# The second forward factor of a global filter network: cosine and sine products in sixteen 32x32 tiles, two steps a run

## The chip, the cores and the metric

One core of a Trainium2 chip runs the whole program. The metric is the device time of one execution in microseconds (us). Three runs of the kernel before gave 2619.46, 2620.3 and 2620.4 us; the median is 2620.3 us.

## What is computed

The reference, cut to what matters, for 8 batches of 3008 tokens with 256 channels:

```python
X = np.fft.rfft(x, axis=1)                 # x: (8, 3008, 256)
Y = X * (filt_r + 1j * filt_i)[None]       # 1505 frequencies x 256 channels
y = np.fft.irfft(Y, n=3008, axis=1)
h = y.reshape(24064, 256) @ w_in           # 256 -> 2048
g = np.where(h > 0, h, np.exp(np.minimum(h, 0)) - 1)
out = g @ w_out                            # 2048 -> 256
```

So every batch passes through a frequency filter (forward transform, product with a complex filter, inverse transform) and then through two dense layers with an ELU between them. All of it is in 32-bit floats.

## The kernel before

**The transform.** 3008 is 47 times 64. The forward transform has a first factor over 64 points (`a_unit`) and a second over 47 points (`b_unit`); the inverse has the second factor back (`bi_unit`) and the first back (`n_unit`). Between the factors the data goes through DRAM to be laid out anew: `z_write` and `z_read` before `b_unit`, `y_write` and `y_read` after `bi_unit`. The second factor works on 32 columns of the first, four at a time, so there are 8 steps g of a batch (`NG` = 8). The cosine and sine parts are folded: 24 rows of sums and 24 rows of differences for each of two parts.

**A `b_unit` of before.** One step g. Sixteen matmuls with weights of 48 rows x 32 columns (`fb`) write the real part into the PSUM bank `psr` and the imaginary one into `psi`. The 48 rows hold a cosine and a sine product that the matmul itself adds. VectorE then multiplies with the filter straight out of PSUM (`products`, L328 to L331, four instructions of 128x512), and GpSimd adds and subtracts the results (L385 to L390). After every second step comes a `bi_unit` over both: 16 matmuls of 24 rows x 32 columns with 512 moving columns, one for each 32x32 tile of the array (`tile_position`), into all four banks (`pv`), which ScalarE copies out (L412).

**The dense layers.** They run by Strassen's scheme, with 7 instead of 8 products. An item is a quarter of the hidden width for one group of tokens; there are 8 x 6 x 4 = 192. Its seven up-steps (`s1`, `s2`, `s6`, `s5`, `s7`, `s3`, `s4`, line L494) multiply with `w_in`, its seven down-steps (L576) with `w_out`. Each step is two fp32 matmuls of 256 columns, which the trace shows as four records.

**The order of the work is written by hand.** The loop runs over quads i. Quad i holds the up-steps of item i and the down-steps of item i-1, interleaved by a string of U and D:

```python
for k in "UUDUDDU":                       # "DUUDUDDU" if i in opens
    ...
for fn, a in plan.get((i, 0), ()):        # place 0: the middle of the quad
    fn(*a)
for k in "DUUDUDD":                       # "DUUDUD" if i in opens
    ...
for fn, a in plan.get((i, 1), ()):        # place 1: its end
    fn(*a)
```

The transform of the next batch is put into this stream by `at(quad, place, fn, ...)`. Below, "quad n" is a quad's place within a batch's 24 (`PER`), that is `t + n` in the code. Every engine takes its instructions in this order.

Before, the eight `b_unit`s stand at the ends of quads 9, 10, 12, 13, 15, 16, 18 and 19, the `bi_unit`s at the ends of 11, 14, 17 and 20. A quad in `opens` begins with a down-step; these were quads 3, 5, 8, 12, 15, 18 and 21. Other work in place 0 or 1 that matters here: `c_unit` (four more VectorE sums of a finished group, L592) in place 0 of quads 5, 9, 13, 17 and 21; `o_unit` (two VectorE transposes, L614) in place 0 of quads 6, 10, 14, 18 and 22; `n_unit` in place 0 of quads 8, 12 and 16. At the end of quads 12, 16 and 20 a finished group adds three VectorE sums (L592).

**PSUM.** Four banks (`po`) hold the down-steps' sums. The other four go round in a list, `banks`:

```python
banks = [0, 1, 2, 3]

def bank(name, shape=(P, 2, D)):
    i = banks.pop(0)
    return i, psM.tile(list(shape), FP32, tag="m%d" % i, name=name)
```

Whoever takes a bank waits until all reads of its last content are done. An item takes its first bank in `s1` (key "s"), a second in `s2` (key "a"), a third in `s7` (key "d"). `s7`'s result is read by VectorE (`add("b22", ...)`, L502 with `phd`), and `s4` then accumulates onto the same bank, so it waits for that read.

Of the kernel before, what the change touches and what calls it, by code (L numbers as in the profile page):

```python
# [11 lines left out]
FP32 = mybir.dt.float32  # L12
U32 = mybir.dt.uint32
AXT = mybir.ActivationFunctionType
# [12 lines left out]
P = 128  # L27
# [14 lines left out]
def _make_tables():  # L42
# [53 lines left out]

    fb, bb = np.zeros((P, 2, 2, 32)), np.zeros((P, 2, 4, 32))
    for r in (LO, HI):  # L100
        fb[r, :, 0, :24] = gb[r, :, 0:24]
        fb[r, 0, 1, 1:24] = gb[r, 0, 24:47]
        fb[r, 1, 1, :24] = gb[r, 1, 24:48]
    for o in range(0, P, 32):
        for p, (t, c) in enumerate(((gr, 0), (gr, 24), (gi, 0), (gi, 24))):
            bb[o:o + 24, 0, p, :24] = t[0:24, 0, c:c + 24]

    bb[0:24, 1, 0, :24], bb[0:24, 1, 1, :24] = gr[0:24, 1, 0:24], gr[24:48, 1, 24:48]
    bb[0:24, 1, 2, :24], bb[0:24, 1, 3, :24] = gi[24:48, 1, 0:24], gi[0:24, 1, 24:48]
    pairs = np.concatenate([fb.reshape(P, P), bb.reshape(P, 2 * P)], 1)  # L110
    lie = np.concatenate([2 * np.arange(24), 2 * np.arange(24) + 1])
    gb[:, :, lie] = gb[:, :, :48].copy()
    for t in (gr, gi):
# [15 lines left out]
def kernel(  # L129
# [16 lines left out]
    def pool(name, bufs, **kw):  # L146
        return ctx.enter_context(tc.tile_pool(name=name, bufs=bufs, **kw))
# [4 lines left out]
    sdp = pool("sdp", 2)  # L152
    tnp = pool("tnp", 2)
    t1p = pool("t1p", 3)
    t2p = pool("t2p", 2)
    sp = pool("sp", 1)
    qp = pool("qp", 1)
    t3p = pool("t3p", 1)
# [5 lines left out]
    psO = pool("psO", 1, space=PSUM)  # L164
    psM = pool("psM", 1, space=PSUM)

    pairs = glob.tile([P, 3 * P], FP32, name="pairs")
    fb = pairs[:, 0:P].rearrange("p (v c k) -> p v c k", v=2, c=2)
    bb = pairs[:, P:3 * P].rearrange("p (v a i) -> p v a i", v=2, a=4)

    w_in, w_out = ([glob.tile([P, 7, 2, P], FP32, name="%s%d" % (n, i)) for i in range(4)] for n in ("wi", "wo"))

    fbufs = [glob.tile([P, 2, 2, D], FP32, name="f%d" % i) for i in range(FBUFS)]
    edges = glob.tile([P, 2], FP32, name="edges")
    fd = fdp.tile([NG, 2, 48, 2, 2, D], FP32, name="fd")
    fp = fdp.tile([NG, 4, 24, 2, 2, D], FP32, name="fp")

    xs, tas, tns, t1s, t2s, ss, t3s, t4s, zs, yds, ys, g_of, po_of, cs_, sds = ({} for _ in range(15))

    def raw(src, row, ap, col=0):  # L180
        return bass.AP(tensor=src.tensor, offset=src.offset + row * D + col, ap=ap)
# [98 lines left out]

    def t_first(g):

        pool, tag = (t4p, "t4") if g % 4 > 1 else (t2p, "t2")
        t = t2s[0, g] = pool.tile([P, 4, D], FP32, tag=tag, name="t2")
        for j in range(2):
            i = j + 2 * (g % 2 if g < 4 else 0)
            ps = psO.tile([P, 2, 256], FP32, tag="po%d" % i, name="po%d" % i)
            for u in range(2):
                k = 4 * g + 2 * j + u
                for dh in range(2):  # L290
                    nc.tensor.transpose(ps[0:ROWS, u, ts(dh, P)], zt[k // 16][dh][:, ts(k % 16, ROWS)], eye)
            nc.scalar.activation(out=t[0:ROWS, 2 * j:2 * j + 2, :], in_=ps[0:ROWS], func=AXT.Copy)
# [10 lines left out]
            nc.sync.dma_start(z[r], t[HALVES[r]])  # L303

    def z_read(b, g):
        t = t2s[b, g] = t2p.tile([P, 4, D], FP32, tag="t2", name="t2")
        for p, r in enumerate((0, 24, 64, 88)):
            k = p * K2 + 4 * g
            nc.sync.dma_start(t[r:r + 24].rearrange("i u d -> i (u d)"), zs[b][:, k:k + 4, :].rearrange("i u d -> i (u d)"))

    def f_read_first(g, t):
        for a, r in enumerate((LO, HI)):
            nc.gpsimd.dma_start(t[r].rearrange("p c u d -> p (c u d)"), fd[g, a].rearrange("q c u d -> q (c u d)"))

    def f_read(b, g):
        t = fbufs[(b * NG + g) % FBUFS]
        for a in range(4):
            nc.gpsimd.dma_start(t[32 * a:32 * a + 24].rearrange("p c u d -> p (c u d)"),
                                fp[g, a].rearrange("q c u d -> q (c u d)"))
# [47 lines left out]


    def b_unit(b, g):
        t = t2s.pop((b, g))  # L370
        f = fbufs[(b * NG + g) % FBUFS]
        (i0, re), (i1, im) = (bank(n) for n in ("psr", "psi"))
        for c in range(2):
            for a in range(4):
                for ps, k in ((re, LO), (im, HI)):
                    nc.tensor.matmul(ps[32 * a:32 * a + 32, c, :], fb[k, 1 if g == a == 0 else 0, c, :], t[k, a, :],  # L376
                                     start=True, stop=True)
        sr, si = (sp.tile([P, 2, D], FP32, tag=n, name=n) for n in ("sr", "si"))
        if g % 2 == 0:
            ss[b, g] = qp.tile([P, 4, 2, D], FP32, tag="z", name="zs")  # L380
        z = ss[b, g - g % 2][:, :, g % 2]
        p, q = z[:, 0:2], z[:, 2:4]
        products(re, im, f, sr, si, p, q)
        banks.extend((i0, i1))
        nc.gpsimd.tensor_tensor(out=sr, in0=sr, in1=p, op=ALU.add)  # L385
        nc.gpsimd.tensor_tensor(out=p[:, 0], in0=sr[:, 0], in1=sr[:, 1], op=ALU.add)
        nc.gpsimd.tensor_tensor(out=p[:, 1], in0=sr[:, 0], in1=sr[:, 1], op=ALU.subtract)
        nc.gpsimd.tensor_tensor(out=si, in0=si, in1=q, op=ALU.add)
        nc.gpsimd.tensor_tensor(out=q[:, 0], in0=si[:, 0], in1=si[:, 1], op=ALU.subtract)
        nc.gpsimd.tensor_tensor(out=q[:, 1], in0=si[:, 0], in1=si[:, 1], op=ALU.add)  # L390
        if g == 0:

            nc.gpsimd.tensor_copy(out=p[0:32], in_=sr[0:32])
            for i in range(2):
                nc.gpsimd.tensor_copy(out=q[0:32, i], in_=si[0:32, 1 - i])

# [233 lines left out]
    def w_fetch(k, queue=nc.gpsimd):  # L632
        q, j = divmod(k, 4)

        if k in (3, 4):
            wd = t2p.tile([P, 4, D], FP32, tag="t2", name="wd").rearrange("p u d -> p (u d)")
        elif k in (10, 11):
            wd = t1p.tile([P, XC, D], FP32, tag="t1", name="wd").rearrange("p u d -> p (u d)")
        elif k in (6, 7, 8, 9):
            wd = xp.tile([P, 2, 2, D], FP32, tag="xc", name="wd").rearrange("p k u d -> p (k u d)")  # L640
        else:
            wd = fbufs[{5: 0, 12: 1, 13: 2, 14: 0, 15: 1}.get(k, k)].rearrange("p c u d -> p (c u d)")
        wd = wds[k] = wd.bitcast(U32).rearrange("p (a w) -> p a w", w=2)
        if j < 2:
            srcs = [moe_w_in.bitcast(U32)[ts(j, P), ts(q, 1024)]]
        else:
            srcs = [moe_w_out.bitcast(U32)[ts(4 * q + 2 * (j - 2) + i, P), :] for i in range(2)]
        for i, s in enumerate(srcs):
            n = 512 // len(srcs)
            queue.dma_start(wd[:, ts(i, n), :].rearrange("p a w -> p (a w)"), s)  # L650
# [79 lines left out]
    def f_pairs(c, u):  # L730

        src = fd.rearrange("g a q c u d -> (g a) q c u d")[:, :, c, u, :]
        dst = fp.rearrange("g (a u) k c h d -> (g a) u k c h d", u=2)[:, u, :, c, :, :]
        nc.gpsimd.dma_start(dst[:, :, 0, :], src[:, 0:48:2, :])
        nc.gpsimd.dma_start(dst[:, 1:24, 1, :], src[:, 1:46:2, :])
        nc.gpsimd.dma_start(dst[:, 0, 1, :], src[:, 47, :])
        if u == 0:
            nc.gpsimd.dma_start(dst[0, :, 1, :], src[0, 1:48:2, :])

    with tc.manual_schedule():  # L740


        with tc.tile_pool(name="boot", bufs=1) as bp:
# [3 lines left out]
            gs = bp.tile([P, 3, 2, 64], FP32, name="gs")  # L747
            gr, gi = gs[:, 1], gs[:, 2]
            zq = qp.tile([P, 4, 2, D], FP32, tag="z", name="zq")
            pqs = [[(sp if i == 0 else bp).tile([P, 2, D], FP32, name="s%s" % n, **({"tag": "s" + n} if i == 0 else {}))  # L750
                    for n in "ri"] +
                   [zq[:, 0:2, i], zq[:, 2:4, i]] for i in range(2)]
            t3f = t3p.tile([P, 2, 4, D], FP32, tag="t3", name="t3")
            zt[0] += [bp.tile([P, 16 * ROWS], FP32, name="zt%d" % i) for i in range(2)]

# [114 lines left out]
        for c in range(2):  # L870
            for u in range(2):
                at(1 + 2 * c + u, 0, f_pairs, c, u)
        for i, f in enumerate(fbufs):
            at(3 + i, 1, nc.vector.memset, f, 0.0)
        for b in range(B):
            t = (b - 1) * PER
            if b > 0:
                for c, s in enumerate((2, 2, 4, 4, 7, 7)):
                    at(t + s, 0, x_unit, b, c)
                    if c % 2 == 0:  # L880
                        opens.add(t + s + 1)
                        at(t + s, 1, a_unit, b, c)
                    nb, nxt = (b, c + XBUFS) if c + XBUFS < NXC else (b + 1, c + XBUFS - NXC)
                    if nb < B:
                        at(t + s, 1, x_load, nb, nxt)
                    at(t + s, 1, z_write, b, c)
                for g in range(NG):
                    s = t + 9 + g + g // 2
                    at(s, 1, b_unit, b, g)
                    at(s - 2, 1, f_read, b, g)  # L890
                    at(s - 2, 1, z_read, b, g)
                    if g % 2:

                        opens.add(s + 2)
                        at(s + 1, 1, bi_unit, b, g - 1)
                        at(s + 1, 1, y_write, b, g - 1)
            for m, (s, place) in enumerate(((23, 0), (25, 1), (29, 1), (32, 0), (36, 0), (40, 0))):
                if b > 0 or m > 0:
                    at(t + s - 2, 0, tn_read, b, m)
# [8 lines left out]
        for i in range(-PER, len(items) + 3):  # L908
            ups, up_tail = up_steps(*items[i]) if 0 <= i < len(items) else ((), None)
            downs, down_tail = down_steps(*items[i - 1]) if 1 <= i <= len(items) else ((), None)  # L910
            ups, downs = list(ups), list(downs)
            for k in "DUUDUDDU" if i in opens else "UUDUDDU":
                s = ups if k == "U" else downs
                if s:
                    s.pop(0)()
            for fn, a in plan.get((i, 0), ()):
                fn(*a)
            for k in "DUUDUD" if i in opens else "DUUDUDD":
# [41 lines left out]
```

## Time and profile before

| | |
|---|---|
| profiled execution: span, its only time on the page | 2618.7 us |
| runs (three), median | 2620.3 us |
| TensorE matmul busy | 2569.9 us, 98% |
| VectorE busy | 1852.8 us, 71% |
| ScalarE busy | 1504.0 us, 57% |
| GpSimd busy | 486.9 us, 19% |
| TensorE clock granted | 0.994 of full on average |

PE is TensorE's matmul, PEld its weight load, DVE is VectorE, ACT ScalarE, POOL GpSimd, SP SyncE, which only issues DMAs. "L328" is line 328 of the kernel. Of the profiled execution the page gives the span and no other time; the runs' median lies 1.6 us above that span. The chain that ended last is the path of waits and work that set the end. Busy shares are means over the whole program: within a quad an engine can be much fuller.

### The profile page before, as it was taken

The page shows a single profiled execution, that of the slowest core. Times are in us where ns is not written, and L with a number is a line of the kernel's source. Part 1 is how long each engine was busy: PE and PEld are TensorE (multiplying, and loading weights), DVE is VectorE, ACT ScalarE, POOL GpSimd, SP SyncE. Part 2 cuts the span into 40 slices and gives each one's busy share as a digit, 9 for nine tenths or more (in the row PEclk, how much of TensorE's full clock was granted, in tenths as well). Part 3 has the DMA queues.
Part 4 walks back from the last instruction along what each step waited for, and adds up shares of the span by engine and source line. Part 5 has one row for each costly group of instructions (what it writes and reads, how often), then busy time and mean ns, then how long its engine had stood idle before and what let it go on. Part 6 is the DMA issues. An engine that isn't in the chain of part 4 may idle for free.

```text
span 2618.7 us, 41226 instructions
## 1 busy us (share of the span) xinstructions
PE 2569.9 (98%) x15300; PEld 2220.2 (85%) x15300; DVE 1852.8 (71%) x3203; ACT 1504.0 (57%) x2622; POOL 486.9 (19%) x669
## 2 busy tenths in 40 slices
PE   6799999999999999999999999999999999999998
PEld 4688889888898888988889888998889888898887
DVE  6876776677666776777667767677677667766666
ACT  7665555655555555555555555555555555555554
POOL 5102330024100331004300134002330023300000
PEclk9899999999999999999999999999999999999999
DMA  9544222432224232333314331143321332210010
GB/s 296 169 115 105 63 63 55 117 83 70 66 62 115 63 92 48 82 90 80 79 45 104 83 98 45 45 111 96 86 61 40 87 85 63 63 41 20 22 28 17
DMA packets 228840, 206.51 MB, mean 79 GB/s; under 512 B 130962, under 2 KB 194674, under 8 KB 228640
## 3 DMA queue, kind: packets, MB, share of 16 engines
q1 hardware_dynamic: 211328, 166.90, 25.4%
q0 software_dynamic: 15856, 36.25, 4.9%
q8 instruction: 121, 1.98, 0.3%
q10 hardware_dynamic: 1456, 0.72, 0.1%
q14 instruction: 79, 0.65, 0.1%
HBM read 131.91 MB, written 78.17 MB: 80 GB/s over the span
## 4 chain that ended last, share of the span: by engine, by line
PE 96%; DMA 0%; DVE 0%; ACT 0%; issue 0%; DVEq 0%; SPq 0%; ACTq 0%
PE po L576 44%; PE phs L494 25%; PE phd L494 12%; PE pha L494 6%; PE psn L443 3%; PE psr L376 2%; PE psa L228 2%; PE pv L409 1%; PE po L324 0%; DMA yd<-t 0%; PE psi L376 0%; DMA t<-yd 0%; PE psr L324 0%; DVE c L592 0%; PE psi L324 0%
## 5 line engine op out<-in xcount | busy, mean ns | idle before, releaser
L576 PE MATMUL po<-g,wo 128*128 128x256 f32 (+1 forms) x5376 | 1306.1, 376 | 0.0
L576 PEld LDWEIGHTS po<-g,wo 128*128 128x128 f32 x5376 | 1016.2, 190 | 139.1 <-issue 20.0
L505 ACT ACTIVATE g<-phs 128x512 f32<-128x512 f32 (+1 forms) x576 | 339.3, 589 | 819.2 <-PE phs L494 819.1
L502 DVE TENSOR_TENSOR g<-phd,g 128x512 f32<-128x512 f32 (+1 forms) x384 | 259.4, 675 | 413.3 <-ACT e L512 322.2
L512 ACT ACTIVATE e<-e 128x512 f32<-128x512 f32 (+1 forms) x768 | 477.2, 621 | 24.3
L516 DVE SCALAR_TENSOR_TENSOR g<-e,g 128x512 f32<-128x512 f32 (+1 forms) x576 | 400.5, 695 | 1.3 <-ACT e L512 1.3
L494 PE MATMUL phs<-y,wi 128*128 128x256 f32 (+1 forms) x1536 | 394.5, 380 | 0.0
L494 PE MATMUL phs<-ys,wi 128*128 128x256 f32 (+1 forms) x1536 | 387.9, 375 | 1.5 <-ACT g L505 1.5
L511 ACT ACTIVATE e<-g 128x512 f32<-128x512 f32 (+1 forms) x576 | 353.2, 613 | 35.7 <-DVE g L502 26.6
L494 PEld LDWEIGHTS phs<-y,wi 128*128 128x128 f32 x1536 | 284.9, 191 | 55.1 <-issue 11.5
L494 PEld LDWEIGHTS phs<-ys,wi 128*128 128x128 f32 x1536 | 291.9, 190 | 34.9 <-ACT g L505 2.5
L385 POOL TENSOR_TENSOR sr<-sr,zs 128x512 f32<-128x512 f32 x56 | 71.3, 1273 | 1131.7 <-DVE zs L330 1131.7
L516 DVE SCALAR_TENSOR_TENSOR g<-e,phs 128x512 f32<-128x512 f32 (+1 forms) x192 | 129.9, 677 | 128.5 <-ACT e L512 128.5
L511 ACT ACTIVATE e<-phs 128x512 f32<-128x512 f32 (+1 forms) x192 | 112.9, 588 | 147.7 <-PE phs L494 147.7
L494 PE MATMUL phd<-ys,wi 128*128 128x256 f32 (+1 forms) x768 | 194.6, 376 | 0.0
L494 PE MATMUL phd<-y,wi 128*128 128x256 f32 (+1 forms) x768 | 193.8, 375 | 0.0
L494 PE MATMUL pha<-y,wi 128*128 128x256 f32 (+1 forms) x768 | 193.8, 375 | 0.0
L494 PEld LDWEIGHTS phd<-ys,wi 128*128 128x128 f32 x768 | 145.4, 190 | 19.0 <-DVE g L502 3.0
L494 PEld LDWEIGHTS pha<-y,wi 128*128 128x128 f32 x768 | 146.1, 190 | 16.3
L494 PEld LDWEIGHTS phd<-y,wi 128*128 128x128 f32 x768 | 146.1, 190 | 16.2
L502 DVE TENSOR_TENSOR g<-pha,g 128x512 f32<-128x512 f32 (+1 forms) x192 | 129.2, 673 | 40.5 <-PE pha L494 40.2
L553 DVE TENSOR_TENSOR g<-g,g 128x512 f32<-128x512 f32 (+1 forms) x192 | 130.7, 681 | 6.7
(129 smaller groups left out, 2356.5 us busy)
## 6 DMA issues: line engine op xcount, KB each, us to landing
yd<-t SPq DMA_DIRECT2D x127, 192.0 KB
t<-yd SPq DMA_DIRECT2D x190, 128.0 KB
z<-t SPq DMA_DIRECT2D x84, 256.0 KB
f<-fp POOLq DMA_DIRECT2D x224, 96.0 KB, 3.1
t<-z SPq DMA_DIRECT2D x224, 96.0 KB
out_dram<-o SPq DMA_DIRECT2D x632, 32.0 KB
tn<-tn_t SPq DMA_DIRECT2D x48, 256.0 KB
xc<-in_x_dram SPq DMA_DIRECT2D x84, 128.0 KB
```

What stands on the lines that cost most here:

```text
L228: nc.tensor.matmul(p[o:o + 64, u, :], w[r, u, o:o + 64], src[r, u, :], start=True, stop=True)
L376: nc.tensor.matmul(ps[32 * a:32 * a + 32, c, :], fb[k, 1 if g == a == 0 else 0, c, :], t[k, a, :], start=True, stop=True)
L385: nc.gpsimd.tensor_tensor(out=sr, in0=sr, in1=p, op=ALU.add)
L443: nc.tensor.matmul(ps[:, ts(q, P)], t[:, i - 4 * m, ds(dh * P, P)], w[:, i - 4 * m, :], start=True, stop=True)
L494: nc.tensor.matmul(ps[:, a, 0:h], w_in[q][:, COMBO[n], a, :], y[n], start=start and a == 0, stop=True, skip_group_check=True)
L502: nc.vector.tensor_tensor(out=g[o], in0=i0, in1=i1, op=ALU.add)
L505: nc.scalar.activation(out=g[o], in_=i0, func=AXT.Copy)
L511: nc.scalar.activation(out=e, in_=src, func=AXT.Relu, scale=-1.0)
L512: nc.scalar.activation(out=e, in_=e, func=AXT.Exp, scale=-1.0)
L516: nc.vector.scalar_tensor_tensor(out=g[n], in0=es[n], scalar=1.0, in1=src, op0=ALU.subtract, op1=ALU.max)
L553: nc.vector.tensor_tensor(out=b12, in0=b22, in1=b12, op=ALU.subtract)
L576: nc.tensor.matmul(po[i][:, u, 0:h], w_out[q][:, COMBO[n], a, :], g[n][:, a, :], start=q == 0 and a == 0 and n in (1, 3, 6, 4), stop=True, ...
```

## The change

- `b_unit` now takes two steps g and g+1 in one run: 16 matmuls, each 24 rows x 32 columns on a tile of its own, with 512 moving columns (20 matmuls for the first pair, whose lone column has other weights). Cosine and sine products come out apart in four PSUM banks: c, s, ci, si. The pairs' units stand at the ends of quads 9, 12, 15 and 18.
- ScalarE copies c and si out; four VectorE instructions form c+s, c-s, si+ci and si-ci. For the first pair (g = 0) VectorE also copies one column out of each of the four banks. The banks go back into the list in the order c, si, s, ci.
- The products with the filter, now from SBUF, are eight VectorE instructions a pair instead of eight out of PSUM. `re_unit` does four of them and four GpSimd instructions in the quad after (10, 13, 16, 19), `im_unit` the other four and four in the quad after that (11, 14, 17, 20). Both stand in a new place 2, behind the third step of a quad.
- The quads after a `b_unit` and after a `bi_unit` are opened by a down-step: quads 10, 13, 16 and 19 join 12, 15, 18 and 21.
- The filter is read in pairs in place 0 of the quad before the unit, and `z_read` in pairs two quads before. `t2`, the filter buffers and `rs` become tiles of fixed place; 2 of the 3 filter buffers are used.

The core of the diff:

```diff
     def b_unit(b, g):
-        (i0, re), (i1, im) = (bank(n) for n in ("psr", "psi"))
-        for c in range(2):
-            for a in range(4):
-                for ps, k in ((re, LO), (im, HI)):
-                    nc.tensor.matmul(ps[32 * a:32 * a + 32, c, :], fb[k, 1 if g == a == 0 else 0, c, :], t[k, a, :],
-                                     start=True, stop=True)
...
-        products(re, im, f, sr, si, p, q)
-        banks.extend((i0, i1))
-        nc.gpsimd.tensor_tensor(out=sr, in0=sr, in1=p, op=ALU.add)
...
+        pf = [bank("pf") for _ in range(4)]
+        both = [(a, p, slice(1 if g == a == 0 else 0, 2), 0) for a in range(4) for p in range(4)]
+        if g == 0:
+            both = [(0, p, slice(0, 1), 1) for p in range(4)] + both
+        for a, p, js, v in both:
+            r = slice(32 * p, 32 * p + 24)
+            nc.tensor.matmul(pf[p][1][32 * a:32 * a + 32, js, :], fb[r, v, :], t2[r, js, a, :],
+                             start=True, stop=True, tile_position=(32 * p, 32 * a))
+        t = rs[b, g] = sp.tile([P, 4, 2, D], FP32, tag="r", name="r")
+        c, s, ci, si = (ps for _, ps in pf)
+        for k, ps in ((1, c), (3, si)):
+            nc.scalar.activation(out=t[:, k], in_=ps, func=AXT.Copy)
+        for k, ps in ((0, s), (2, ci)):
+            nc.vector.tensor_tensor(out=t[:, k], in0=t[:, k + 1], in1=ps, op=ALU.add)
+            nc.vector.tensor_tensor(out=t[:, k + 1], in0=t[:, k + 1], in1=ps, op=ALU.subtract)
+        if g == 0:
+            for k, ps in ((0, c), (1, s), (3, ci), (2, si)):
+                nc.vector.tensor_copy(out=t[0:32, k, 0, :], in_=ps[0:32, 0, :])
+        banks.extend(pf[p][0] for p in (0, 3, 1, 2))
+
+    def re_unit(b, g):
+        t, f = rs[b, g], fall[:, 0:2]
+        z = ss[b, g] = qp.tile([P, 4, 2, D], FP32, tag="z", name="zs")
         for c in range(2):
...
+            nc.vector.tensor_tensor(out=z[:, 2 + c], in0=t[:, c], in1=f[:, :, 0, c, :], op=ALU.mult)
+            nc.vector.scalar_tensor_tensor(out=z[:, c], in0=t[:, 2 + c], scalar=-1.0, in1=f[:, :, 1, c, :],
+                                           op0=ALU.mult, op1=ALU.mult)
+        for c in range(2):
+            nc.gpsimd.tensor_tensor(out=z[:, 2 + c], in0=z[:, 2 + c], in1=z[:, c], op=ALU.add)
+        for c, op in ((0, ALU.add), (1, ALU.subtract)):
+            nc.gpsimd.tensor_tensor(out=z[:, c], in0=z[:, 2], in1=z[:, 3], op=op)
...
+    def im_unit(b, g):
+        t, f, z = rs.pop((b, g)), fall[:, 0:2], ss[b, g]
+        for c in range(2):
+            nc.vector.tensor_tensor(out=t[:, c], in0=t[:, c], in1=f[:, :, 1, c, :], op=ALU.mult)
+            nc.vector.tensor_tensor(out=t[:, 2 + c], in0=t[:, 2 + c], in1=f[:, :, 0, c, :], op=ALU.mult)
+        for c in range(2):
+            nc.gpsimd.tensor_tensor(out=t[:, c], in0=t[:, c], in1=t[:, 2 + c], op=ALU.add)
+        for c, op in ((0, ALU.subtract), (1, ALU.add)):
+            nc.gpsimd.tensor_tensor(out=z[:, 2 + c], in0=t[:, 0], in1=t[:, 1], op=op)
...
-                for g in range(NG):
-                    s = t + 9 + g + g // 2
+                for g in range(0, NG, 2):
+                    s = t + 9 + 3 * g // 2
+                    opens.update((s + 1, s + 3))
+                    for k in (g, g + 1):
+                        at(s - 1, 0, f_read, b, k)
+                        at(s - 2, 1, z_read, b, k)
                     at(s, 1, b_unit, b, g)
...
+                    at(s + 1, 2, re_unit, b, g)
+                    at(s + 2, 2, im_unit, b, g)
+                    at(s + 2, 1, bi_unit, b, g)
+                    at(s + 2, 1, y_write, b, g)
...
-            for k in "DUUDUDDU" if i in opens else "UUDUDDU":
+            for n, k in enumerate("DUUDUDDU" if i in opens else "UUDUDDU"):
...
+                if n == 2:
+                    for fn, a in plan.get((i, 2), ()):
+                        fn(*a)
```

## The prediction

> **What bounds the kernel now.** I read the page's busy line and chain first, then the matmul timeline around a `b_unit` and a `bi_unit`, then VectorE's timeline in the quads that the change touches, the busy times quad by quad, and the waits.
>
> ```profile
> PE 2569.9 (98%) x15300; PEld 2220.2 (85%) x15300; DVE 1852.8 (71%) x3203; ACT 1504.0 (57%) x2622; POOL 486.9 (19%) x669
> ...
> PE 96%; DMA 0%; DVE 0%; ACT 0%; issue 0%; DVEq 0%; SPq 0%; ACTq 0%
> ```
>
> TensorE is the bound. So an edit is worth what it takes out of TensorE's stream, less every new wait in it, because TensorE's steps run in order. The units in that stream, batch 2 (g = 3, then the `bi_unit` after it):
>
> ```profile
> 593.11 1.89 PE L576 MATMUL po<-g,wo 128*128 128x256 f32 x8
> 594.92 0.40 PE L376 MATMUL psr<-t,pairs 48*32 48x256 f32 x1
> ...
> 595.95 1.13 PE L494 MATMUL phs<-y,wi 128*128 128x256 f32 x4
> 596.92 1.03 PE L494 MATMUL pha<-y,wi 128*128 128x256 f32 x4
> ...
> 606.41 1.89 PE L576 MATMUL po<-g,wo 128*128 128x256 f32 x8
> 608.23 1.14 PE L409 MATMUL pv<-zs,pairs 24*32 24x512 f32 x32
> 609.30 1.13 PE L576 MATMUL po<-g,wo 128*128 128x256 f32 x4
> 610.27 1.05 PE L494 MATMUL phs<-y,wi 128*128 128x256 f32 x4
> ```
>
> A step (x4) takes 0.863 us start to start, a quad of 14 steps 12.09. The two down-steps from 593.11 would end at 594.84; the next ordinary step starts at 595.95 and is 0.97 long instead of 0.863. One `b_unit` thus costs 1.11 + 0.11 = 1.22 us. By the same count the `bi_unit` costs 608.14 to 609.30 plus 0.11 = 1.27 us; that of a first pair, with 40 records, 1.42.
>
> VectorE runs behind TensorE. A `b_unit` of quad 9 (g = 0) and what VectorE does of it:
>
> ```profile
> 539.44 0.40 PE L376 MATMUL psr<-t,pairs 48*32 48x256 f32 x1
> ...
> 542.47 0.69 DVE L328 TENSOR_TENSOR sr<-psr,f 128x512 f32<-128x512 f32 x1
> ...
> 544.87 0.68 DVE L502 TENSOR_TENSOR g<-pha,g 128x512 f32<-128x512 f32 x1
> ```
>
> It comes to the unit only 3.03 us after the unit began, since the tail of the item before is queued ahead; four 128x512 instructions then take 2.40, 0.60 each. In the other quads the delay is longer. Busy times of quads 13, 16 and 17:
>
> ```profile
> 582.38:594.92 12.54, 12.54 (x64) 10.48 (x56) 12.28 (x22) 6.37 (x11) 6.11 (x6) 1.00 0.11 33
> ...
> 622.63:636.70 14.07, 14.07 (x80) 12.37 (x73) 9.20 (x16) 8.36 (x16) 5.33 (x6) 1.00 0.10 29
> 637.73:650.01 12.28, 12.28 (x65) 10.57 (x57) 11.90 (x22) 6.02 (x11) 7.19 (x9) 1.00 0.00 0
> ```
>
> The columns are length, then PE, PEld, DVE, ACT, POOL. VectorE's 71% hides two quads with `c_unit` that are already full: 12.28 of 12.54 and 11.90 of 12.28. In quad 13 TensorE already waits for it:
>
> ```profile
> 591.41 0.68 DVE L502 TENSOR_TENSOR g<-phd,g 128x512 f32<-128x512 f32 x1
> 592.14 1.13 PE L494 MATMUL phd<-ys,wi 128*128 128x256 f32 x4
> ...
> PEld phd L494 <- DVE g L502: 3.0, 8, 0.4
> ```
>
> `s4` was due at 591.97 and starts at 592.14, after the read of `s7`'s bank ends at 592.09.
>
> **The change, part by part**, for one batch, times 7 (batch 0 is filtered by other functions).
>
> *Tiling.* The new unit has the form of the `bi_unit` (16 tiles, 24x32, 512 columns), so I price it 1.27; its moving rows are two runs of 256 columns instead of one, and no row shows that to cost. The first pair has 20 matmuls, two of them on the same tile in four cases, as its `bi_unit` has: 1.42, up to 1.7 as they stand first. Before 8 x 1.22 = 9.76, after 3 x 1.27 + 1.42 = 5.23: a gain of 4.53, **-31.7 us** (-26 to -33).
>
> *Banks, first pair (quad 10).* The unit holds all four banks. `s1` of quad 10, behind one down-step, takes c's bank, and for g = 0 that bank has a last reader on VectorE: the one-column copy, queued behind the tail and the four sums. The copy starts 3.03 + 2.40 = 5.43 us after the unit's start and takes about 0.35 (estimate: 256-column sums take 0.42, start to start 0.34). `s1` can start at 5.8; without the wait it would at 1.23 (matmuls of a 40-record `bi_unit`) + 0.97 = 2.2. Everything behind `s1` stands for 3.6 us; the last copy (si, for `s2`'s bank) ends at 6.8, when `s1` is done. **+25.2 us** (23 to 27).
>
> *Banks, other pairs.* c and si have only ScalarE as a reader. It copies at 0.60 each and is free then: `bi_unit`'s copies wait 0.79 for the matmuls. `s1` comes one down-step later, as behind the `bi_unit`, where it starts on time (610.27). Cost 0; were that copy late, 0.6 for 21 units is 12.6. But a unit at the end of quads 12, 15 and 18, which end with only one down-step behind `s4`, now needs `s4`'s bank, whose reader ends at 581.45 for a unit due at 581.35: 0.15 x 3, **+3 us** (0 to 5).
>
> *VectorE.* A pair has 12 instead of 8 instructions of 128x512, 4 x 0.60 x 28 = 67 us in all. Where it is idle they are free: quad 16 has a hole of 4.01 us before `s7`'s sum, quads 10 and 19 enough. Quad 13: `add("b11")`, queued behind the four sums, ends 7.87 after the unit's start (589.22), `re_unit` adds 4 x 0.60 to 0.70 = 2.5, the `c_unit` takes 2.19 as now, the sum of `s7` 0.65: 13.2. `s4` is due at 1.07 + 0.11 + 12 x 0.863 = 11.53. The wait is 1.67 instead of 0.17, **+10.5 us** (5 to 14). Quad 17 loses the unit in front of it and gets `im_unit` for `products`, while quad 16 now opens with a down-step, so that its tail ends one step nearer to the boundary or past it. VectorE comes to `products` 4.1 us behind the stream now (L328 at 640.71, the steps end at 636.61), 0.86 later then (quad 12, opened so and with the same three sums, shows 586.23 against 581.26, 4.97): 4.96 + 0.6 + 2.45 + 2.2 + 0.65 = 10.86, against `s4` due at 11 x 0.863 = 9.5: 1.36, **+9.5 us** (3 to 14). Quads 11, 14 and 20 come out at 7.9 to 9.5: no wait.
>
> *GpSimd and `bi_unit`.* `im_unit`'s GpSimd work must end before the quad does, 12.18 us after its start. It begins when VectorE has two products, 5.9 (quads 11, 20), 6.1 (14), 6.8 (17), and takes 4 x 1.27 to 1.45, in a first pair 2 x 0.39 more: it ends between 11.0 and 12.4, and in quad 17 TensorE is late anyway. 0 (0 to 8). `re_unit`'s part has a quad of cover.
>
> *Moves at no cost.* Two more ScalarE copies a pair lie in holes (819 us before L505). The filter reads (8 issues of 0.50 on POOL's queue, landing in 3.1) now follow `im_unit` and have over 10 us. `z_read` goes ahead of a `y_write` on SP's queue instead of behind it, earlier. Were the cover gone, a filter read would cost its landing, 3.1 us a pair.
>
> *Clock.* A row of the start-up bears on the 3.6 us of standstill: after an idle time of 3.94 us
>
> ```profile
> 29.50:33.30 3.80, 3.75 (x16) 3.48 (x16) 2.56 (x5) 0.66 (x2) 0.65 (x2) 0.50 1.03 396
> ```
>
> the granted clock was 0.50; after 1.02 and 1.83 it was not lowered. In the records the clock changes in multiples of 3.41 us; a drop would cost half of one, 1.7. I take one drop in seven: **+2 us** (0 to 12). The Trainium skill ("TensorE: Matmul & The Clock Gate", Why this matters for your kernels) wants no matmul gap over about 3 us; by it all seven standstills would drop, 12 in place of 2.
>
> *Sum.* -31.7 + 25.2 + 3 + 10.5 + 9.5 + 2 = +18.5 on a span of 2618.7, 2637.2; with the 1.6 that the median lies above the span, **2639**.
>
> The skill also speaks against the change: "TensorEngine Tiling (Array Packing)", PSUM Bottleneck, says that tiling speeds up TensorE but not the emptying of PSUM. Read strictly, each run's four VectorE sums, 2.4 us, would stand in the stream, 67 us; the rows let three of four pairs hide them.
>
> **Rivals.**
>
> *Quad-10 wait absent (faster).* Place: `s1` of quad 10. Price: 25.2, so 2614. If TensorE finds c's bank free there, by a reading of the list or of VectorE's queue that I have wrong, the rest is -6.7. It decides from a standstill under about 1 us; above that the sum is positive. For it: ScalarE alone would free the bank in time. Against: 3.03 us in all seven batches. Should quads 13 and 17 fit as well, 2594.
>
> *Only quads 13 and 17 fit.* Their two terms vanish, 20: 2619, no change. For it: products from SBUF could run a little faster than 0.60. Against: 12.28 of 12.54.
>
> *GpSimd late (slower).* If its instructions stretch beside a full VectorE (1.45 against 1.27 is seen) and `bi_unit` waits 1 us in all 28: +28, 2667.
>
> *Tiles not side by side.* If the 16 tiles ran in two rounds, a run would cost 0.86 more, 24 in all less what quad 10 hides (6): 2657.
>
> **How the numbers follow.** This kernel's measurement can tell about 0.2%, 5.2 us, from no change. Forecast 0.63, wait absent 0.13, only 13 and 17 fit 0.10, GpSimd late 0.09, tiles 0.05. Faster: 0.13 and half of the no-change case's spread below it, 0.04, make 0.17; same 0.08, its other 0.06 and 0.02 from the forecast's low end; slower 0.75. Ends of the forecast's own terms, not all at once: 2622 to 2656. The range reaches to the first rival's 2614 and takes in the no-change case and the tiles: 2613 to 2660, which leaves out a part of the first rival, most of the GpSimd case and the forecast's far ends, under 0.2.
>
> **What would show it.** Right: the new unit at 1.07 us of matmul; an idle TensorE of about 3.6 us once a batch before `phs`, put down to a VectorE copy; `phd` of quads 13 and 17 waiting 1.3 to 1.7 for L502's line; VectorE full there. Wrong: no standstill in quad 10; a unit longer than 1.5; `pv` waiting for GpSimd; a VectorE with room in quad 13.

## The result, and the profile after

The changed kernel takes 2738.9 us (median of 4 runs), the one before 2619.9 on the same chip: 1.045 times as long, with a 95% interval of 1.0435 to 1.0464. The profiled execution has a span of 2738.0 us against 2618.7, 119.3 more. The prediction had the direction, at a sixth of the size.

The page of the changed kernel, its busy line and its chain:

```profile
PE 2605.1 (95%) x14460; PEld 2233.7 (82%) x14460; DVE 2053.2 (75%) x3342; ACT 1535.0 (56%) x2678; POOL 491.4 (18%) x564
...
PE 80%; DVE 12%; issue 2%; ACT 2%; POOL 1%; DMA 0%; DVEq 0%; ACTq 0%
```

TensorE has 840 instructions fewer and is busy for 35 us longer, so something makes its instructions slow; and VectorE, at 0% of the chain before, now holds 12% of it. The waits of TensorE (waiting tile and line, releaser; total us, times, longest):

```profile
PE phd L518 <- DVE g L526: 52.0, 22, 3.6
PE phs L518 <- DVE r L392: 23.9, 7, 3.4
...
PE pv L433 <- POOL zs L419: 7.6, 7, 1.4
```

The first is `s4` behind VectorE's read of `s7`'s bank: per batch 3.62 in quad 13, 3.27 in quad 17 and 0.42 in quad 20, most of it. The second is `s1` of quad 10 behind the one-column copies. The third is the `bi_unit` of quad 11 behind GpSimd.

TensorE's timeline in batch 2, first pair and second pair:

```profile
557.00 1.72 PE L381 MATMUL pf<-t,pairs 24*32 24x256 f32 x40
558.65 1.13 PE L600 MATMUL po<-g,wo 128*128 128x256 f32 x4
563.20 2.04 PE L518 MATMUL phs<-y,wi 128*128 128x256 f32 x4 [3.42 <-DVE r L392]
565.04 1.91 PE L518 MATMUL pha<-y,wi 128*128 128x256 f32 x4
...
607.95 1.28 PE L381 MATMUL pf<-t,pairs 24*32 24x512 f32 x32
609.17 1.13 PE L600 MATMUL po<-g,wo 128*128 128x256 f32 x4
610.13 1.04 PE L518 MATMUL phs<-y,wi 128*128 128x256 f32 x4
```

The unit of the second pair costs what was forecast (607.95 to 609.17, and 0.96 to the next step): by the table below 1.41 us, the forecast's 1.27 and 0.14 in which its fourth tile waits for `s4`'s bank. In quad 10 `s1` stands for 3.42 us, but then comes what the prediction hardly counted: its four records take 2.04 us instead of about 1.03, and the next step's 1.91. Four windows of that stretch show why (length, then busy PE, PEld, DVE, ACT, POOL, then the granted clock):

```profile
559.00:562.10 3.10, 0.78 (x4) 0.35 (x2) 3.00 (x6) 0.62 (x2) 0.00 (x0) 0.99 0.00 0
562.10:565.50 3.40, 2.30 (x6) 1.89 (x7) 1.94 (x5) 0.22 (x1) 0.00 (x0) 0.50 0.00 0
565.50:568.90 3.40, 3.40 (x10) 2.69 (x9) 1.84 (x4) 0.38 (x1) 0.00 (x0) 0.50 0.00 0
568.90:572.00 3.10, 3.10 (x16) 2.74 (x15) 3.10 (x5) 0.60 (x1) 2.27 (x2) 1.00 0.00 0
```

After a window with 0.78 us of matmul the clock is halved for two periods. In the stretch from 200 to 2600 us there are 24 such drops, over 30 periods of 3.41 us. TensorE stood idle for 9.0 of these 102.4 us (the first halved window above has 1.1 of that), and the other 93.4 did half the work of a full clock: 46.7 us are lost. Before had none there. With the idle time of TensorE in that stretch (83.5 us, before 0) the loss is 130.2; the 10.9 us by which it exceeds the 119.3 were won elsewhere.

**VectorE in quad 13.** Its timeline before the late read of `s7`'s bank, and TensorE's line that waits for it:

```profile
617.26 0.68 DVE L399 TENSOR_TENSOR zs<-r,fall 128x512 f32<-128x512 f32 x1
617.86 1.76 DVE L400 SCALAR_TENSOR_TENSOR zs<-r,fall 128x512 f32<-128x512 f32 x1
619.54 0.41 DVE L616 TENSOR_TENSOR k<-k,c 128x256 f32<-128x256 f32 x1
619.99 1.37 DVE L616 TENSOR_TENSOR c<-c,k 128x256 f32<-128x256 f32 x1
621.29 0.41 DVE L616 TENSOR_TENSOR c<-po,k 128x256 f32<-128x256 f32 x1
621.62 1.15 DVE L616 TENSOR_TENSOR c<-k,k 128x256 f32<-128x256 f32 x1
622.69 0.68 DVE L526 TENSOR_TENSOR g<-phd,g 128x512 f32<-128x512 f32 x1
```

```profile
623.42 2.04 PE L518 MATMUL phd<-ys,wi 128*128 128x256 f32 x4 [3.62 <-DVE g L526]
```

The product of L400 takes 1.76 us instead of the 0.68 of the one ahead of it; of the `c_unit`'s sums the one with a PSUM input (`po`) takes 0.41; of the three with two SBUF inputs two take 1.37 and 1.15, and one (`k<-k,c`) 0.41. In this time GpSimd runs `re_unit`'s sums:

```profile
617.51 1.56 POOL L403 TENSOR_TENSOR zs<-zs 128x512 f32<-128x512 f32 x1 [22.54 <-DVE zs L400]
619.70 1.38 POOL L403 TENSOR_TENSOR zs<-zs 128x512 f32<-128x512 f32 x1 [0.63 <-DVE zs L400]
621.16 2.73 POOL L405 TENSOR_TENSOR zs<-zs 128x512 f32<-128x512 f32 x2
```

The three long instructions began while one of these sums was running, and `k<-k,c` in the pause from 619.07 to 619.70.

This is where the theory comes from that most of the runs below ask about: **GpSimd's sums stretch VectorE's instructions with two SBUF inputs, that makes TensorE wait, and most of the longer waits halve the clock.** The rivals: the tiled units lower the clock by themselves, or the waits come from the data that VectorE and GpSimd hand to each other.

The table gives, from the traces, the time from the first matmul of `s6` in quad n to that of the next quad's, as a mean over the seven batches (an opened quad moves 0.87 us from its own row to the row before):

| quad | before | after | e1 | e3 | e7 | e8 | e9 |
|---|---|---|---|---|---|---|---|
| 9 | 13.31 | 20.73 | 14.80 | 20.91 | 14.80 | 14.80 | 14.80 |
| 10 | 13.31 | 11.41 | 11.93 | 11.49 | 11.22 | 12.60 | 11.93 |
| 11 | 14.37 | 17.14 | 17.51 | 14.37 | 14.37 | 18.19 | 14.73 |
| 13 | 13.57 | 16.62 | 17.69 | 12.35 | 12.35 | 12.75 | 15.71 |
| 17 | 14.24 | 19.21 | 18.01 | 14.99 | 14.99 | 15.52 | 18.86 |
| 20 | 14.24 | 15.71 | 15.71 | 14.22 | 14.22 | 15.70 | 15.08 |
| 9 to 20 | 164.8 | 181.8 | 176.4 | 169.1 | 162.7 | 172.5 | 172.6 |

### The profile page after: what moved, and what is told of

It is laid out like the page before. It is cut to its first block, busy times and chain, and to the rows that moved or that the text cites. A ratio compares the mean times of both kernels' runs of the same rounds, so it can differ in the third digit from the quotient of the medians.

```text
span 2738.0 us, 39630 instructions
## 1 busy us (share of the span) xinstructions
PE 2605.1 (95%) x14460; PEld 2233.7 (82%) x14460; DVE 2053.2 (75%) x3342; ACT 1535.0 (56%) x2678; POOL 491.4 (18%) x564
## 4 chain that ended last, share of the span: by engine, by line
PE 80%; DVE 12%; issue 2%; ACT 2%; POOL 1%; DMA 0%; DVEq 0%; ACTq 0%
PE po L600 36%; PE phs L518 21%; PE phd L518 10%; PE pha L518 5%; PE psn L467 3%; DVE g L540 2%; DVE g L526 2%; PE psa L232 1%; PE pv L433 1%; DVE r L413 1%; DVE c L616 1%; ACT e L536 1%; ACT e L535 1%; DVE g L577 1%; POOL zs L417 1%
## 5 line engine op out<-in xcount | busy, mean ns | idle before, releaser
L600 PE MATMUL po<-g,wo 128*128 128x256 f32 (+1 forms) x5376 | 1334.6, 381 | 0.0
L600 PEld LDWEIGHTS po<-g,wo 128*128 128x128 f32 x5376 | 1026.9, 193 | 169.8 <-issue 44.2
L529 ACT ACTIVATE g<-phs 128x512 f32<-128x512 f32 (+1 forms) x576 | 338.6, 588 | 803.1 <-PE phs L518 803.1
L536 ACT ACTIVATE e<-e 128x512 f32<-128x512 f32 (+1 forms) x768 | 477.2, 621 | 24.3
L540 DVE SCALAR_TENSOR_TENSOR g<-e,g 128x512 f32<-128x512 f32 (+1 forms) x576 | 445.5, 774 | 5.7 <-ACT e L536 5.0
L518 PE MATMUL phs<-y,wi 128*128 128x256 f32 (+1 forms) x1536 | 399.3, 383 | 23.9 <-DVE r L392 23.9
L518 PEld LDWEIGHTS phs<-y,wi 128*128 128x128 f32 x1536 | 293.6, 195 | 65.6 <-issue 26.5
L403 POOL TENSOR_TENSOR zs<-zs 128x512 f32<-128x512 f32 x56 | 80.1, 1431 | 1072.2 <-DVE zs L400 789.4
L518 PE MATMUL phd<-ys,wi 128*128 128x256 f32 (+1 forms) x768 | 203.8, 389 | 52.0 <-DVE g L526 52.0
L518 PE MATMUL pha<-y,wi 128*128 128x256 f32 (+1 forms) x768 | 201.0, 386 | 0.0
L577 DVE TENSOR_TENSOR g<-g,g 128x512 f32<-128x512 f32 (+1 forms) x192 | 130.7, 681 | 6.7
```

The lines of the kernel that those rows point to most:

```text
L403: nc.gpsimd.tensor_tensor(out=z[:, 2 + c], in0=z[:, 2 + c], in1=z[:, c], op=ALU.add)
L518: nc.tensor.matmul(ps[:, a, 0:h], w_in[q][:, COMBO[n], a, :], y[n], start=start and a == 0, stop=True, skip_group_check=True)
L529: nc.scalar.activation(out=g[o], in_=i0, func=AXT.Copy)
L536: nc.scalar.activation(out=e, in_=e, func=AXT.Exp, scale=-1.0)
L540: nc.vector.scalar_tensor_tensor(out=g[n], in0=es[n], scalar=1.0, in1=src, op0=ALU.subtract, op1=ALU.max)
L577: nc.vector.tensor_tensor(out=b12, in0=b22, in1=b12, op=ALU.subtract)
```

## The experiments

**e1: the bank wait of quad 10 taken away.** For the first pair ScalarE saves the lone columns of c and si, so that no reader of these banks stands in VectorE's queue.

```diff
-        for k, ps in ((1, c), (3, si)):
+        ln = fall[0:32, 2, 0]
+        for n, (k, ps) in enumerate(((1, c), (3, si))):
             nc.scalar.activation(out=t[:, k], in_=ps, func=AXT.Copy)
+            if g == 0:
+                nc.scalar.activation(out=ln[:, n, :], in_=ps[0:32, 0, :], func=AXT.Copy)
...
-            for k, ps in ((0, c), (1, s), (3, ci), (2, si)):
-                nc.vector.tensor_copy(out=t[0:32, k, 0, :], in_=ps[0:32, 0, :])
+            for k, lone in ((0, ln[:, 0, :]), (1, s[0:32, 0, :]), (3, ci[0:32, 0, :]), (2, ln[:, 1, :])):
+                nc.vector.tensor_copy(out=t[0:32, k, 0, :], in_=lone)
```

> The changed kernel, except that for g = 0 ScalarE saves the lone columns of c and si and so is the only reader of the two banks that s1 and s2 of quad 10 take. Theory A (waits, each lengthened by the halved clock that follows it): the 3.42 us standstill of quad 10 goes, and with it the two halved clock windows (6.83 us at half speed, 3.4 lost): 7 x 6.8 = 48 us less than the changed kernel, about 2691. Rival B (the clock falls because of the tiled matmuls, not because of the waits): the halved windows near the first pair's unit stay, only 7 x 3.4 = 24 us go, about 2715.

Measured: 2706.3 us, 1.0328 times before (1.0311 to 1.0345), 32.6 less than the changed kernel. Its span is 2703.0, and its waits are

```profile
PE phd L521 <- DVE g L529: 58.5, 35, 3.6
...
PE pv L436 <- POOL zs L422: 9.9, 7, 1.4
```

The wait of `phs` is gone. By the table quads 9 and 10 lose 5.4 us per batch, 38 in all, of which 24 were the wait itself. (Quads 11 and 13 take 1.4 more per batch and quad 17 takes 1.2 less, which nearly cancels.) So a standstill of 3.4 us cost half as much again as its own length. (Quad 10 of e1 has a new wait of 0.44 us; against e7, without it, the difference is 6.1 a batch.) The time lies between the two expectations and doesn't separate them, but the trace does: none of the nine drops of the clock that are left follows a `b_unit`.

**e2: `re_unit` behind the sum of `s7`.** The products are queued behind the read that `s4` waits for.

```diff
-                    at(s + 1, 2, re_unit, b, g)
+                    at(s + 1, 3, re_unit, b, g)
...
-            for k in "DUUDUD" if i in opens else "DUUDUDD":
+            for n, k in enumerate("DUUDUD" if i in opens else "DUUDUDD"):
...
+                if n == 1:
+                    for fn, a in plan.get((i, 3), ()):
+                        fn(*a)
```

> The changed kernel with re_unit moved behind the up-step s7, so that VectorE forms s7's sum, for which s4 waits, before it. Theory A: the wait of s4 in quad 13 (3.6 us and a halved clock window after it, 1.7) goes, 7 x 5.3 = 37 us less, some of it given back as the later GpSimd work of re_unit pushes im_unit's: 2702 to 2720. The wait in quad 17 (3.3) stays. Rival C (VectorE is simply overfull over the whole stretch): the wait moves to the next quad and the time falls by less than 10 us.

Measured: 2823.5 us, 1.077 (1.0754 to 1.0786), the worst of all. The expectation was wrong. Quad 13 itself came out as hoped (13.28 instead of 16.62), but the wait moved:

```profile
PE phd L518 <- DVE g L526: 62.8, 26, 5.8
PE phs L518 <- ACT g L529: 54.7, 30, 1.9
PE phs L518 <- DVE r L392: 23.9, 7, 3.4
```

The new second line is `s6` of the next quad, 28 times 1.90. The products and GpSimd's sums now lie beside the tail (`elu_max`, L576, L577), which has two SBUF inputs too; there L576 takes 1.75 us in batch 2, and 0.88 on average over the program against 0.69 in the changed kernel. ScalarE's `exp` waits for the tail, and the `keep` copy of the next item (L529), which frees `s6`'s bank, is queued behind it. In quad 17 the wait of `s4` grew to 5.8.

**e3: the changed kernel without GpSimd's part.** The sums and one-column copies of `re_unit` and `im_unit` on GpSimd are left out; everything else is as in the changed kernel.

```diff
-        for c in range(2):
-            nc.gpsimd.tensor_tensor(out=z[:, 2 + c], in0=z[:, 2 + c], in1=z[:, c], op=ALU.add)
-        for c, op in ((0, ALU.add), (1, ALU.subtract)):
-            nc.gpsimd.tensor_tensor(out=z[:, c], in0=z[:, 2], in1=z[:, 3], op=op)
...
```

> The changed kernel without GpSimd's sums and copies in re_unit and im_unit (they are left out of the computation). Theory A (GpSimd's work stretches VectorE's instructions that read and write SBUF only): the stretched ones (1.76, 1.37, 1.15 us in quad 13) fall to 0.6 or less, s4's waits go from 3.6 to about 1.6 in quad 13 and from 3.3 to about 1.4 in quad 17, bi_unit waits for nothing; with the clock windows that no longer halve 45 to 65 us less, 2675 to 2695. Rival C (the queue is long by the number of its instructions alone): s4's waits stay at 3.6 and 3.3, only bi_unit's waits and their windows go, 15 to 20 us less, about 2720.

Measured: 2654.2 us, 1.0122 (1.0107 to 1.0137): 84.7 less than the changed kernel, more than either side expected. Its waits:

```profile
PE phs L506 <- DVE r L392: 23.9, 7, 3.4
...
PE phd L506 <- DVE g L514: 9.6, 14, 0.9
```

The wait of quad 10 is untouched, that of `pv` is gone, and that of `s4` is 0.86 in quad 13 and 0.51 in quad 17, under the 1.67 and 1.36 of the prediction. So VectorE's extra work alone fits these quads better than forecast.

**e4: the bank wait alone, in the kernel before.** One line changes which bank comes next after the first `b_unit`, so that `s1` of quad 10 needs a bank that VectorE reads last; nothing is tiled.

```diff
-        banks.extend((i0, i1))
+        banks[0 if g == 0 else len(banks):0] = (i0, i1)
```

> The kernel before with one line changed: for g = 0 the two banks of b_unit go back to the front of the list, so that s1 of quad 10 waits for two of the VectorE products (about 3.2 us). Nothing is tiled anew. Theory A: a wait of 7 x 3.2 = 22 us, and the clock halves after each for one or two windows of 3.41 us, 12 to 24 us more: 2654 to 2666. As the prediction had it (one drop in seven): about 2644. Rival B (the clock falls for the tiling): no window is halved, 2642.

Measured: 2659.1 us, 1.0142 (1.0127 to 1.0157), 37.2 more than before. One line, seven standstills of 3.34 us, 23.4 in all, and a halved clock after each of the seven. Windows of its stretch in batch 2:

```profile
544.41:547.82 3.41, 0.33 (x16) 0.00 (x0) 3.38 (x6) 0.00 (x0) 0.00 (x0) 0.91 0.01 2
547.82:551.23 3.41, 3.13 (x8) 2.53 (x9) 1.33 (x3) 0.60 (x1) 2.45 (x3) 0.50 0.00 0
```

There are no tiled `b_unit`s here: the clock falls from the standstill alone.

**e5 and e6: the same wait, shorter.** As e4, but one down-step (e5) or two (e6) stand ahead of `s1` in quad 10.

```diff
 # e5
                     at(s, 1, b_unit, b, g)
+                    if g == 0:
+                        opens.add(s + 1)
 # e6, besides
-            for k in "DUUDUDDU" if i in opens else "UUDUDDU":
+            for k in "DDUUDUDU" if i % PER == 10 and i > -1 else "DUUDUDDU" if i in opens else "UUDUDDU":
```

> As e4_before_bank, with quad 10 opened by a down-step, so that s1 comes 0.97 us later to the same bank: its wait falls from 3.3 to about 2.2 us. Theory A says the clock halves when about half of a 3.41 us stretch of a fixed grid is idle (in the runs so far drops follow stretches with under 1.8 us of matmul, where no tiled unit stands beside the wait): 7 x 2.2 = 15 us of waiting and a drop after most of them, 4 to 7 times 1.7: 2642 to 2648. If only standstills over 3 us halve it: 2635.

> As e5_before_bank_d, with two down-steps ahead of s1 in quad 10: the wait falls to about 1.3 us. Theory A: 7 x 1.3 = 9 us and hardly a drop, since a grid stretch then has 2 us of matmul or more: 2629 to 2632. If every standstill halves the clock: 2641.

Measured: e5 2652.5 us, 1.0122 (1.0102 to 1.0142), 31.9 more than before; e6 2637.6, 1.0065 (1.0045 to 1.0085), 17.0 more. Both lie above what was expected. The wait is 2.28 us in e5 and 1.42 in e6. The same two windows, first of e5:

```profile
544.41:547.82 3.41, 1.24 (x12) 0.68 (x4) 3.38 (x7) 0.00 (x0) 0.00 (x0) 1.00 0.01 2
547.82:551.23 3.41, 3.18 (x9) 2.43 (x10) 1.18 (x2) 0.60 (x1) 2.60 (x3) 0.66 0.00 0
```

and of e6:

```profile
544.41:547.82 3.41, 2.86 (x40) 1.77 (x28) 3.34 (x6) 0.41 (x1) 0.00 (x0) 1.00 0.00 0
547.82:551.23 3.41, 2.42 (x10) 1.90 (x11) 2.06 (x5) 0.60 (x1) 1.84 (x2) 1.00 0.01 2
```

A wait of 2.28 us lowered the clock in six of seven batches, one of 1.42 in none. In e5 the one that did not had 1.75 us of matmul in its period, the six that did 1.11 to 1.14. (The windows above are cut by hand and may straddle two periods.) e6 shows what a wait costs without any clock drop: by the measure of the table quads 9 and 10 together take 2.07 us more than before, 14.5 in seven batches, for seven waits of 1.42 and seven pieces of 0.09 beside them, 10.6. That leaves 0.56 a wait. (The rest of the 17.0 lies ahead of these quads, in the start-up.) TensorE's first weights after the wait are not loaded ahead: in batch 2 their load begins at 548.68 and the matmul at 548.71. What part of the 0.56 that makes was not measured.

**e7: e1 and e3 together.** Neither the bank wait nor GpSimd's sums and copies; the tiled units stand as in the change.

> e1_lane_act and e3_no_gpsimd together (GpSimd's sums and copies of re_unit and im_unit are left out). Theory A: what is left are waits of s4 of 0.9 and 0.5 us in quads 13 and 17 and no halved clock, so the gain of the tiling shows: e3's 2654 less 7 x 3.4 of waiting and 22 of clock, about 2608, 0.5% under the kernel before. Rival B (tiled matmuls lower the clock): halved windows stay and it is not under 2620.

Measured: 2604.4 us, 0.9941 (0.9925 to 0.9958), with a span of 2601.3. One kind of wait is left, and no period of lowered clock between 200 and 2590 us:

```profile
PE phd L509 <- DVE g L517: 9.6, 14, 0.9
```

So the gain of the tiling is there, and tiled units by themselves do not lower the clock. By the table the first unit costs 1.84 us and the others 1.41 where eight of 1.22 stood: 9.76 - 6.07 = 3.69 a batch, 25.8 in all. Of this, the wait that is left takes 9.6 back, 0.86 in each quad 13 and 0.51 in each quad 17. The time is not one to be had, since GpSimd's sums are missing.

**e8: e1, with the `c_unit` split.** Two of the `c_unit`'s three sums with two SBUF inputs, those that were long in quad 13, move to the end of the quad, behind the read that `s4` waits for.

```diff
-            cs_[b, m] = c, lambda: [add(*r) for r in rest]
+            cs_[b, m] = c, lambda n: [add(*rest[j]) for j in ((0, 2), (1, 3))[n]]
...
-                at(t + PER + 4 * m + 5, 0, c_unit, b, m)
+                for n in range(2):
+                    at(t + PER + 4 * m + 5, n, c_unit, b, m, n)
```

> e1_lane_act with the two SBUF-only sums of c_unit (stretched to 1.37 and 1.15 us in quads 13 and 17) moved from the middle to the end of the quad, so that s7's sum comes about 2.5 us sooner. Theory A: s4's waits fall from 3.6 to about 1.1 and from 3.3 to about 0.8, below what halves the clock; some of it comes back in quads 14 and 18, where VectorE starts later: 2655 to 2680, against 2706 of e1_lane_act. Rival C (VectorE overfull): the waits only move on to quads 14 and 18, 2695 or more.

Measured: 2676.7 us, 1.0214 (1.0199 to 1.023), 29.7 less than e1.

```profile
PE phd L521 <- DVE g L529: 43.1, 42, 1.9
...
PE pv L436 <- POOL zs L422: 9.9, 7, 1.4
```

Now no wait is longer than 1.9 us, and instead of 9 drops over 15 periods there are 4 over 4. The waits are only spread: 42 small ones sum to 43.1. This is the fastest version with all of the work in it, and it is still 56 us slower than the kernel before.

**e9: GpSimd busy, with nobody waiting for it.** As e7, but GpSimd has eight sums a pair of the same size at the same places, written to a spare tile that nobody reads.

```diff
-        for c in range(2):
-            nc.gpsimd.tensor_tensor(out=z[:, 2 + c], in0=z[:, 2 + c], in1=z[:, c], op=ALU.add)
...
+        for c in (0, 1, 0, 1):
+            nc.gpsimd.tensor_tensor(out=fall[:, 2, 1], in0=z[:, 2 + c], in1=z[:, c], op=ALU.add)
```

> e7_lane_no_gpsimd with four GpSimd sums put back in re_unit and four in im_unit, of the same size, at the same places and reading the same tiles, but writing to a spare tile that nobody reads. So GpSimd is as busy as in e1_lane_act, and no instruction waits for what it makes. Theory A (busy beside VectorE is enough): the SBUF-only VectorE instructions of quads 13 and 17 are stretched again, s4's waits come back to 3.3 to 3.6 us with a halved clock window after each, 14 x (2.7 + 1.7) = 62 us, while bi_unit waits for nothing: 2660 to 2680. Rival D (VectorE lost the time to waits for GpSimd's results): about 2605, as e7.

Measured: 2678.9 us, 1.022 (1.0202 to 1.0238): 74.5 more than e7, for sums whose results no one takes.

```profile
PE phd L513 <- DVE g L521: 59.5, 33, 3.6
```

The waits of `s4` are back at those of e1 (58.5). But only seven of the fourteen long ones were followed by half clock, 8 periods in all against 15 in e1, where the expectation had a drop behind each.

Three groups of VectorE's instructions by form, each with its count, its busy us in all and mean ns of one. The changed kernel:

```profile
L400 DVE SCALAR_TENSOR_TENSOR zs<-r,fall 128x512 f32<-128x512 f32 x56 | 68.6, 1225 | 0.0
L616 DVE TENSOR_TENSOR c<-c,k 128x256 f32<-128x256 f32 x40 | 30.3, 756 | 1.4
L616 DVE TENSOR_TENSOR c<-po,k 128x256 f32<-128x256 f32 x120 | 46.6, 416 | 0.7 <-PE po L600 0.7
```

Without GpSimd's sums (e7):

```profile
L403 DVE SCALAR_TENSOR_TENSOR zs<-r,fall 128x512 f32<-128x512 f32 x56 | 38.1, 680 | 0.0
L607 DVE TENSOR_TENSOR c<-c,k 128x256 f32<-128x256 f32 x40 | 17.0, 425 | 1.4
L607 DVE TENSOR_TENSOR c<-po,k 128x256 f32<-128x256 f32 x120 | 46.5, 415 | 0.7 <-PE po L591 0.7
```

With sums to the spare tile (e9):

```profile
L403 DVE SCALAR_TENSOR_TENSOR zs<-r,fall 128x512 f32<-128x512 f32 x56 | 68.3, 1220 | 0.0
L611 DVE TENSOR_TENSOR c<-c,k 128x256 f32<-128x256 f32 x40 | 30.3, 756 | 1.4
L611 DVE TENSOR_TENSOR c<-po,k 128x256 f32<-128x256 f32 x120 | 46.4, 414 | 0.7 <-PE po L595 0.7
```

The instructions with two SBUF inputs take on average 1.8 times as long in e9 as in e7, and as long as in the changed kernel (only some of each group meet GpSimd's sums; a single product then took 1.76 us above); the one with a PSUM input is untouched in all three. So it is GpSimd's running, not its results, that makes `s4` wait. The Trainium skill ("SBUF — State Buffer", Who interferes with whom) has the rule: a VectorE instruction with two SBUF inputs and a GpSimd instruction that reads SBUF contend for a shared port, which the first to start holds to its end; a VectorE instruction with at most one SBUF input, outside its 2-port modes, does not contend. The three groups agree, with 756 against 425 ns and 414 to 416.

## Why the prediction was wrong

| step | predicted, us | measured, us | from |
|---|---|---|---|
| tiling, with the waits at the unit | -31.7 + 3 | -25.8 | e7 |
| bank wait of quad 10 | +25.2 | +23.9 | waits after; e4 +23.4 |
| `s4` in quad 13 | +10.5 | +25.3 (7 x 3.62) | waits after; e3 6.0 |
| `s4` in quad 17 | +9.5 | +22.9 (7 x 3.27) | waits after; e3 3.5 |
| `bi_unit` behind GpSimd | 0 | +7.6 | waits after |
| `s4` in quad 20 | 0 | +3.0 (7 x 0.42) | waits after |
| clock | +2 | +46.7 | 30 halved periods, less their idle time |
| not accounted to a step | 0 | +15.7 | the remainder of 119.3 |

**The tiling** was forecast well in mechanism and size: 16 tiles side by side (1.22 us start to start in the second pair); the rival of tiles in two rounds fell. The first unit (1.84 instead of 1.42) makes the 2.9 us that are missing; the others measured 1.41 against 1.27 + 0.15.

**The bank wait** was forecast to 0.2 us, from the queue of one engine: 3.6 against 3.42. The rival of an absent wait fell. What was missed is what follows the wait.

**The clock** is the term that was wrong most: 45 of the 100 us that the prediction missed. It rested on one row of the start-up with 3.94 us of idle time and two without a drop, 1.02 and 1.83; between them I took "one drop in seven" for 3.6, which no row supported. The trace before even had a nearer row that spoke against it, a wait of 3.33 us in the start-up with two halved periods behind it (the timeline, then two windows):

```profile
70.15 1.97 PE L324 MATMUL psr<-t,once 48*64 48x512 f32 x2 [3.33 <-DVE si L329]
```

```profile
66.40:69.81 3.41, 0.42 (x3) 0.00 (x0) 3.38 (x9) 1.85 (x3) 0.00 (x0) 0.99 0.41 145
69.81:73.22 3.41, 3.07 (x13) 1.37 (x17) 3.41 (x7) 3.38 (x7) 0.00 (x0) 0.50 0.39 94
```

e4 has seven of seven at 3.34, e5 six of seven at 2.28. The rule that the prediction set beside it, of the Trainium skill ("TensorE: Matmul & The Clock Gate", Why this matters for your kernels), speaks of gaps over about 3 us; it would have been the better choice for quad 10, but a wait's length alone does not decide: 2.28 was enough in e5, and 3.27 in quad 17 of e1 was not in six of seven batches (see the last section). The waits of quads 13 and 17 need counting too. The price of one drop was also too low, since several last two periods.

**Quads 13 and 17** were named rightly, but the waits are 2.0 and 1.9 us longer. The failing step is the duration of 0.60 for each product and "2.19 as now" for the `c_unit`: both hold for instructions that run alone or read PSUM (alone, the product of L400 takes 680 ns in e7, and the one from PSUM before 682). The products before read PSUM; the change makes their inputs SBUF, and puts GpSimd's sums for them beside the fullest stretch of VectorE. Without GpSimd the waits are 0.86 and 0.51 (e3), smaller than forecast. That the trace before could have warned is shown by its `c_unit`: there `c<-c,k` takes 0.57 us on average, but `c<-po,k`, of the same shape, 0.42.

**GpSimd and the `bi_unit`** was put at 0 with a range to 8. Only quad 11, the first pair's, waits, 7.6 in all. With clock and restart quads 11 and 20 cost more: their rows are 2.77 and 1.47 us above before, 29.7 in seven batches. The rival "GpSimd late" had its place in part right and its main way wrong: GpSimd's cost reaches TensorE by VectorE far more than by `bi_unit`.

The same sum by place instead, against the kernel without any of these waits (e7 less its two waits), per batch: quad 10 takes 6.1 us, quad 11 2.8, quad 13 5.1, quad 17 4.7, quad 20 1.5 and quad 14 0.2. Over seven batches that is 142.8 of loss. The kernel so compared with lies 24.3 under the one before (14.7 in the table's row 9 to 20, and its waits of 9.6), which leaves 118.5 of the 119.3. So the loss does not sit in a single fault: e1 mends quad 10 and e8 spreads quads 13 and 17, and neither comes near 2620. The pair with the least harm, the fourth (quads 18 to 20), still has 0.44 us more than before in e1.

What stays open: the 0.56 us that a wait costs beyond its length in e6, from which the remainder of 15.7 us may come. That is not shown: in e4, where the clock fell after each wait, nothing of it is left (37.4 us in quads 9 and 10, of which 23.4 are waiting and 13.8 the clock). Open is also why the clock fell after some `bi_unit`s that waited (last section).

## What to carry to other kernels

A wait on the engine that bounds the kernel costs more than its length: count the standstill, the halved clock behind it (here from about 2 us of idle time in one period of the clock on, so that the same wait may or may not bring it), and the restart. When an edit moves an elementwise operand from PSUM to SBUF, price the instruction with GpSimd running beside it, and ask which wait of the bounding engine is queued behind it. Where an engine is full in some quads, moving its work within the quad only moves the wait; look for what it shares with its neighbour before its place.

## What the runs showed of the hardware

- The clock is decided in periods of 3.41 us on a fixed grid: in each run all its changes between 100 and 2590 us lie whole periods apart. In the runs of the kernel before with a longer wait (e4 to e6) a period with up to 1.14 us of matmul was followed by half clock, one with 1.75 was not; over all runs, of the full-clock periods between 200 and 2590 us that hold no tiled matmul, every one under 1.42 us was followed by half clock, none from 1.53 on, and in between both occurred. A standstill of 2.28 us is thus enough where it lies within one period, and one of 3.27 is not where the grid cuts it. That is quad 17 of e1 in batch 2, with 1.43 and 2.13 us of matmul in the two periods:

```profile
669.70:673.11 3.41, 1.43 (x7) 0.92 (x5) 3.38 (x5) 1.23 (x2) 2.70 (x3) 1.00 0.00 0
673.11:676.53 3.42, 2.13 (x10) 1.90 (x11) 3.42 (x5) 1.05 (x2) 3.42 (x6) 1.00 0.10 29
```

  So it was in part luck which waits halved the clock: that of quad 17 did in six of seven batches of the changed kernel and in one of seven of e1.
- The exception is open: after the `bi_unit` of quad 11, the clock fell in some batches though the period before held 1.99 to 2.39 us of matmul (all four drops of e8 are such), and behind the wait of quad 10 it fell three times though the period held 1.63 to 1.82. All of these periods hold a wait and tiled matmuls. In e7, with the same tiled units and no such wait, it never fell. Whether small tiles count for less was not tried.
- VectorE instructions with two SBUF inputs (`c<-c,k`, 128x256) take 425 ns without GpSimd's sums (e7) and 756 on average with them (e9, and the changed kernel), the 128x512 product of L400 680 and 1220 to 1225. A 128x256 sum with one PSUM input takes 414 to 416 in all three.
